# Expert stage of a fused model: float64 conversion on VectorE and ScalarE alone, its stores on SP's queue, row copies on ScalarE, another order of products and another branch form

## The chip, the cores and the metric

The kernel runs on one core of a Trainium2 chip. The metric is the device time of one execution in microseconds; less is better. Engines are named as in the profile: PE multiplies matrices, ACT is ScalarE, DVE is VectorE, POOL is GpSimd, and SP issues most DMAs. ACTq and SPq are the DMA queues that ACT and SP issue on, in the order of their own instructions.

## The reference

Three blocks follow each other: an attention with decay, a mixture of experts in which every token takes 2 of 8, and a gated product with large weights. `moe2_w_a` and its two companions arrive as float64.

```python
x = attention(q, k, v)                      # 1536 tokens, 512 wide
for e in range(8):                          # top 2 of 8 experts for each token
    mask = top2[:, k] == e
    out[mask] += top2_w[mask, k, None] * (np.maximum(x[mask] @ w1[e], 0.0) @ w2[e])   # 512 -> 1024 -> 512
a = x @ w_a                                 # 512 -> 1536, weights float64
b = x @ w_b
return (a * b @ w_out).astype(np.float32)
```

## The kernel before, in words

The attention and the choice of experts take the first 100 us or so. The expert stage, which the change is about, runs until about 450 us, and the gated product takes the rest.

**Products.** Every float32 factor is split into a high and a low part, and a product is three matmuls (`three`, lines 714 to 716): high by high, high by low, low by high. Weights are split as they come: `W.piece` (lines 81 and 82) copies half a unit to the high part on ACT (`whi`), subtracts on DVE (`wlo`), and then has SP load the next raw half. Two raw halves are in memory at a time.

**Experts.** The tokens of an expert are gathered into `xg`, transposed (`xprep`) and split (`xh`, `xl`). For each of 8 slices `f` of the hidden layer, `up` makes 12 matmuls into a PSUM tile `pu`, of which there are two; ACT writes the high part of the relu (`hh` or `hz`, line 747), DVE the low part (line 750). `down` multiplies that slice by the second weights and adds into four PSUM tiles `py0` to `py3`, which exist once. A list `behind` keeps `down` two slices behind `up`. So the last `down` of expert e-1 stands in slice 1 of expert e. Directly behind it `yevac` copies the four `py` tiles to `yt`: two on ACT (line 789), two on DVE (line 787). The next product is `up` of slice 2; the `down` after it writes `py0` again.  In slices 3 to 6 `ytrans` transposes `yt` and POOL scatters the rows to `ytab` in memory. In slice 6 POOL gathers the tokens of the expert after the next.

**Conversion.** Beside this the float64 weights are turned into float32, 36 chunks of 128 x 512: in slices 0, 1, 3, 5 and 7 of an expert, and in more slices of the first two. `wide_load` has SP fetch the words (`wr`). `wide_first` converts the low word on ACT (`wl`, line 592), and on DVE it works out the float32 word from the high one in six operations (lines 593 to 598). One slice later `wide_second` multiplies and adds the low part on POOL (lines 608 and 609), and one slice after that `wide_store` writes the chunk to `wtab` on ACT's queue (line 616). In expert 3, slice 1, SP also sends a list to memory and reads it back in another layout (`last_index`, lines 669 and 672); the second DMA waits for the first.

**Branch.** In expert 0, half of the tokens are worked ahead of a branch: `tc.If(rounds > 0)` (line 971) covers the case that an expert has more tokens than its tiles hold. With these data it isn't entered. All engines read `rounds` and branch.

The program's order is fixed by the code: each engine works its own list in order.

Of the kernel before, what the change touches and what calls it, by code (L numbers as in the profile page):

```python
# [8 lines left out]
F32 = mybir.dt.float32  # L9
# [3 lines left out]
U32 = mybir.dt.uint32  # L13
AF = mybir.ActivationFunctionType
OP = mybir.AluOpType
# [74 lines left out]
def tile_model(ctx: ExitStack, tc: tile.TileContext, q, k, v, w_gate, w_noise, noise, w1, w2,  # L90
               w_a, w_b, w_out, cst, tok, out):
    nc = tc.nc
# [12 lines left out]
    units, wide = [], []  # L105
# [457 lines left out]
    psu = mctx.enter_context(tc.tile_pool(name="psu", bufs=2, space=PSUM, reuse_waits="tile"))  # L563


    LO = float(np.uint32(896 << 20).view(np.float32))
    HI = float(np.uint32(1151 << 20).view(np.float32))
    wide_raw, wide_mid = {}, {}
    wide_n = [0, 0, 0, 0]

# [9 lines left out]
            return zp.tile([128, 512], U32, tag="zl", name="wa")  # L580
        return m2.tile([128, 512], U32, tag="wa", name="wa", bufs=3)

    def wide_first():

        n = wide_n[1]
        if n >= len(wide):
            return
        wr = wide_raw.pop(n)
        hw, lw = wr[:, :, 1], wr[:, :, 0]
        a = wide_word(n)  # L590
        q_, lf = (m2.tile([128, 512], U32, tag=x, name=x, bufs=2) for x in ("wq", "wl"))
        nc.scalar.activation(lf.bitcast(F32), lw, AF.Copy, scale=2.0 ** -52)
        nc.vector.tensor_scalar(a, hw, 0x7FFFFFFF, None, OP.bitwise_and)
        nc.vector.tensor_scalar(q_, hw, 0x7FFFFFFF, 0x3FFFFFFF, OP.bitwise_or, OP.bitwise_xor)
        nc.vector.tensor_scalar(a.bitcast(F32), a.bitcast(F32), LO, HI, OP.max, OP.min)
        nc.vector.tensor_scalar(a, a, 3, 0x7FFFFFFF, OP.logical_shift_left, OP.bitwise_and)
        nc.vector.tensor_tensor(a, a, q_, OP.bitwise_xor)
        nc.vector.tensor_scalar(q_, a, 0xFF800000, None, OP.bitwise_and)  # L598
        wide_mid[n] = (a, q_, lf)
        wide_n[1] += 1  # L600
        wide_load()

    def wide_second():
        n = wide_n[2]
        if n >= wide_n[1]:
            return
        a, q_, lf = wide_mid.pop(n)
        nc.gpsimd.tensor_tensor(lf.bitcast(F32), lf.bitcast(F32), q_.bitcast(F32), OP.mult)  # L608
        nc.gpsimd.tensor_tensor(a.bitcast(F32), a.bitcast(F32), lf.bitcast(F32), OP.add)  # L609
        wide_mid[n] = a  # L610
        wide_n[2] += 1

    def wide_store():
        n = wide_n[3]
        if n < wide_n[2]:
            nc.scalar.dma_start(wide[n][1], wide_mid.pop(n).bitcast(F32))
            wide_n[3] += 1


# [54 lines left out]
    XG, XH, XL, HH, HL, PY, YT, YS = {}, {}, {}, {}, {}, {}, {}, {}  # L674
# [54 lines left out]
    def up(e, f, w=None, keep=False, c=None, wait=False):  # L729
        if not w:  # L730
            v = slice(f % 4 * 128, f % 4 * 128 + 128)
            w = [[x[:, d, v] for d in range(4)] for x in W.tiles[("w1", e, f // 4)]]
        wh, wl = w
        a, b = c or (0, cap(e))
        n = b - a
        pu = psu.tile([128, 512], F32, tag="pu", name="pu")[:, 0:n]
        for d in range(4):
            three(pu, wh[d], wl[d], XH[e][:, d, a:b], XL[e][:, d, a:b], d == 0, d == 3)
        if keep:
            if f % 4 == 0:  # L740
                last[f // 4] = last_half(f // 4)
            HH[e, f], HL[e, f] = last[f // 4][0][f % 4], last[f // 4][1][f % 4]
        elif e == "r":
            HH[e, f], HL[e, f] = (m2.tile([128, 512], U32, tag="wl", name="wl").bitcast(F32R)[:, 0:n] for _ in range(2))
        else:
            HH[e, f], HL[e, f] = hidden(n)
        nc.scalar.activation(HH[e, f], pu, AF.Relu)  # L747

        def low():
            nc.vector.scalar_tensor_tensor(HL[e, f], pu, 0.0, HH[e, f].bitcast(F32), OP.max, OP.subtract)  # L750

        if wait:
            return low
        low()
# [27 lines left out]
    def yevac(e):  # L782
        YT[e] = m1.tile([128, 4, CP], F32, tag="yt", name="yt")
        n = cap(e)
        for m in range(4):
            if m % 2:
                nc.vector.tensor_copy(YT[e][:, m, 0:n], PY[e][m][:, 0:n])
            else:
                nc.scalar.copy(YT[e][:, m, 0:n], PY[e][m][:, 0:n])  # L789

    def scatter(ix, src):
        nc.gpsimd.indirect_dma_start(out=ytab, out_offset=bass.IndirectOffsetOnAxis(ap=ix, axis=0),
# [47 lines left out]
    def count_rounds():  # L840


        cnt = ranks["cnt"]
        nc.vector.tensor_tensor(rr[:, 0:E], cnt, caps, OP.is_gt)
        nc.vector.tensor_tensor(early[:, 1:E], early[:, 1:E], ranks["sel"][0:1, E - 2], OP.mult)
        nc.vector.tensor_reduce(rr[:, 8:9], rr[:, 0:E], AX.X, OP.max)
        nc.vector.tensor_reduce(early[:, 0:1], early[:, 1:E], AX.X, OP.add)
        nc.vector.tensor_reduce(rr[:, 9:10], cnt, AX.X, OP.max)
        nc.vector.scalar_tensor_tensor(rr[0:1, 8:9], few, PA - OFF, rr[0:1, 8:9], OP.is_lt, OP.max)
        nc.vector.scalar_tensor_tensor(rr[0:1, 8:9], early[:, 0:1], 128.0 - OFF, rr[0:1, 8:9], OP.is_gt, OP.max)  # L850
        for i in range(NR):
            nc.vector.tensor_scalar(rr[0:1, i:i + 1], rr[0:1, 9:10], i * CP - OFF, rr[0:1, 8:9], OP.is_gt, OP.mult)
        with nc.allow_low_precision(reason="whole numbers up to 4"):
            nc.vector.tensor_reduce(ri32, rr[0:1, 0:NR], AX.X, OP.add)
# [108 lines left out]
    up(0, 0, c=gb)  # L963
    nc.vector.memset(pofs, -float(CP))
    count_rounds()
    up(0, 1, c=gb)
    down(0, 0, c=gb)
    up(0, 2, c=gb)
    down(0, 1, c=gb)
    rounds = load_rounds()  # L970
    with tc.If(rounds > 0, preferred_fallthrough_block=False):
        more_rounds(rounds)
    xtiles("r")
    W.piece()
# [10 lines left out]

    for e in range(E):
        for f in range(0 if e else 3, NF):
            wide_store()
            wide_second()
            if e == E - 1:  # L990
                up(e, f, keep=True)
            else:
                up(e, f)
                behind.append((e, f))
            if e and 3 <= f < 7:
                ytrans(e - 1, f - 3)
            if behind and (len(behind) > 2 or e == E - 1):
                next_down()
            if e + 1 < E and 0 <= f - 2 - (e == 0) < 4:
                xprep(e + 1, f - 2 - (e == 0))  # L1000
            if e + 2 < E and f == 6:
                gather(e + 2)
            if e == E - 1 and f > 1:
                tile_mm(e, 0, f - 2)
            if e == 2 and f == 1:
                gate()
            if e == 3 and f == 1:
                last_index()
            if e + 1 < E:
                if e or f > 1:  # L1010
                    W.piece()
                if f in (0, 1, 3, 5, 7) or e < 2 and f == 4 or e == 0 and f == 6:
                    wide_first()
            elif f < 6:
                W.piece()
    G0 = [sum(GS[:i]) for i in range(len(GS))]
    YG, X2, ZH, ZL = {}, {}, {}, {}

# [188 lines left out]
```

## Time and profile before

| | |
|---|---|
| median of 3 runs | 790.31 us (787.67 to 790.79) |
| profiled execution | 789.01 us, of which its span is 787.2 us |
| granted TensorE clock, mean | 0.97 |

The span goes from the first to the last instruction; 1.8 us lie around it. The profile gives for each engine its busy time, in windows the clock that TensorE was granted (1.00 is 2.4 GHz, 0.50 is 1.2 GHz), and for each instruction how long its engine stood idle before it and which instruction released it. Line numbers are those of the kernel before.

### The profile page before, as it was taken

Reading aid. Unit: us, or ns where it says so; the run is one execution under the profiler, and the core shown is the slowest. Engines: PE = TensorE matmul, PEld = TensorE weight load, DVE = VectorE, ACT = ScalarE, POOL = GpSimd, SP = SyncE. Lnnn points to the kernel's source line nnn. Section 1 sums busy time; section 2 is a strip of 40 time slices with the busy share of each in tenths; the row PEclk is TensorE's granted clock in tenths of the full one; section 3 lists DMA queues with packets and bytes.
Section 4 is the critical chain, followed back from the end, with each engine's and each line's share of the span. In section 5 each row is a group of like instructions: output and inputs, shape, how many; then the busy total and the mean of one; then the engine's idle time right before and its main releaser. Section 6 shows DMA issues by size and latency. Waiting matters only on the chain. (4 is left out here: it accounts for less than half of the span.)

```text
span 787.2 us, 12000 instructions
## 1 busy us (share of the span) xinstructions
PE 735.6 (93%) x4657; PEld 683.8 (87%) x4657; DVE 433.6 (55%) x800; ACT 281.7 (36%) x524; POOL 215.1 (27%) x164
## 2 busy tenths in 40 slices
PE   8989898979899898979899979999999999999997
PEld 5878787869799887979889859999999999999997
DVE  4587565989778679787887534632222332222211
ACT  3674723335443343535344534421112122111211
POOL 4331131655746446474654210000000000000000
PEclk9999998989999899999999988999999999999999
DMA  9894244776857568576765654602001202000100
GB/s 219 224 263 117 56 143 142 234 214 221 247 200 232 165 216 253 201 235 219 235 211 164 180 188 155 188 1 81 0 1 41 81 1 81 1 1 1 41 1 27
DMA packets 85997, 107.85 MB, mean 137 GB/s; under 512 B 34521, under 2 KB 48089, under 8 KB 85934
## 3 DMA queue, kind: packets, MB, share of 16 engines
q1 hardware_dynamic: 69054, 81.45, 34.5%
q0 software_dynamic: 6272, 13.32, 5.9%
q10 hardware_dynamic: 10608, 12.25, 4.5%
q8 instruction: 38, 0.62, 0.3%
q14 instruction: 25, 0.20, 0.1%
HBM read 84.60 MB, written 22.38 MB: 136 GB/s over the span
## 5 line engine op out<-in xcount | busy, mean ns | idle before, releaser
L714 PE MATMUL ab<-zh,whi 128*128 128x256 f32 (+1 forms) x480 | 146.7, 306 | 0.0
L716 PE MATMUL ab<-zh,wlo 128*128 128x256 f32 (+1 forms) x480 | 146.6, 305 | 0.0
L715 PE MATMUL ab<-zl,whi 128*128 128x256 f32 (+1 forms) x480 | 146.5, 305 | 0.0
L82 DVE TENSOR_TENSOR wlo<-raw,whi 128x1024 fp32r<-128x1024 f32 x82 | 120.1, 1466 | 37.8 <-ACT whi L81 34.3
L1104 DVE TENSOR_TENSOR gf<-ab,bs 128x256 f32<-128x256 f32 (+1 forms) x60 | 28.6, 477 | 179.5 <-PE ab L716 179.4
L714 PE MATMUL pu<-xh,whi 128*128 128x432 f32 (+9 forms) x268 | 96.1, 358 | 7.4 <-issue 3.8
L714 PEld LDWEIGHTS ab<-zh,whi 128*128 128x128 f32 x480 | 92.0, 192 | 2.6
L715 PEld LDWEIGHTS ab<-zl,whi 128*128 128x128 f32 x480 | 91.9, 192 | 2.4
L81 ACT CAST whi<-raw 128x1024 fp32r<-128x1024 f32 x82 | 86.3, 1053 | 18.3 <-DMA raw<-wtab 9.9
L715 PE MATMUL pu<-xl,whi 128*128 128x432 f32 (+9 forms) x268 | 92.6, 346 | 0.0
L716 PE MATMUL pu<-xh,wlo 128*128 128x432 f32 (+9 forms) x268 | 92.4, 345 | 0.0
L716 PEld LDWEIGHTS ab<-zh,wlo 128*128 128x128 f32 x480 | 91.9, 191 | 0.0
L608 POOL TENSOR_TENSOR wl<-wl,wq 128x512 f32<-128x512 f32 x36 | 47.3, 1315 | 100.4 <-DVE wq L598 87.3
L609 POOL TENSOR_TENSOR wa<-wa,wl 128x512 f32<-128x512 f32 x36 | 72.8, 2023 | 2.8
L714 PE MATMUL py<-hh,whi 128*128 128x408 f32 (+8 forms) x160 | 59.3, 370 | 13.6 <-ACT yt L789 8.6
L1103 ACT COPY bs<-ab 128x256 f32<-128x256 f32 (+1 forms) x60 | 24.9, 415 | 122.2 <-PE ab L716 122.2
L1105 ACT CAST gh<-gf 128x256 fp32r<-128x256 f32 (+1 forms) x60 | 27.0, 449 | 107.6 <-DVE gf L1104 107.6
L714 PEld LDWEIGHTS pu<-xh,whi 128*128 128x128 f32 x268 | 52.0, 194 | 9.6 <-issue 4.0
L747 ACT ACTIVATE hh<-pu 128x408 fp32r<-128x408 f32 (+9 forms) x42 | 20.8, 496 | 105.3 <-POOL wa L609 40.6
L714 PE MATMUL po<-whi,gh 128*128 128x512 f32 x144 | 57.9, 402 | 0.0
L715 PE MATMUL py<-hl,whi 128*128 128x408 f32 (+8 forms) x160 | 56.8, 355 | 0.0
L715 PE MATMUL po<-wlo,gh 128*128 128x512 f32 x144 | 56.7, 394 | 0.0
(212 smaller groups left out, 1383.6 us busy)
## 6 DMA issues: line engine op xcount, KB each, us to landing
raw<-in_moe_w SPq DMA_DIRECT2D x64, 512.0 KB, 4.0
wtab<-wa ACTq DMA_DIRECT2D x36, 256.0 KB, 4.1
raw<-wtab SPq DMA_DIRECT2D x18, 512.0 KB, 4.2
wr<-in_moe_w_a SPq DMA_DIRECT2D x12, 512.0 KB, 5.3
wr<-in_moe_w_b SPq DMA_DIRECT2D x12, 512.0 KB, 5.1
wr<-in_moe_w_out SPq DMA_DIRECT2D x12, 512.0 KB, 6.5
yg<-ytab SPq DMA_DIRECT2D x24, 256.0 KB, 3.7
kr<-in_k SPq DMA_DIRECT2D x12, 256.0 KB, 5.1
```

Source lines behind the costliest of these rows:

```text
L81: nc.scalar.copy(hi[:, a:b], raw)
L82: nc.vector.tensor_tensor(lo[:, a:b], raw, hi[:, a:b].bitcast(F32), OP.subtract)
L608: nc.gpsimd.tensor_tensor(lf.bitcast(F32), lf.bitcast(F32), q_.bitcast(F32), OP.mult)
L609: nc.gpsimd.tensor_tensor(a.bitcast(F32), a.bitcast(F32), lf.bitcast(F32), OP.add)
L714: nc.tensor.matmul(ps, ah, bh, start=start, stop=False, skip_group_check=part)
L715: nc.tensor.matmul(ps, ah, bl, start=False, stop=False, skip_group_check=part)
L716: nc.tensor.matmul(ps, al, bh, start=False, stop=stop, skip_group_check=part)
L747: nc.scalar.activation(HH[e, f], pu, AF.Relu)
L1103: nc.scalar.copy(bs, ps["b"])
L1104: nc.vector.tensor_tensor(gf, ps["a"], bs, OP.mult)
L1105: nc.scalar.copy(GH[g, f][:, 0:n], gf)
```

## The change

- The conversion: ACT takes the absolute value of the high word as a float, scaled (`AF.Abs`, into `wa`), and converts the low word as before. DVE has six operations: sign, minimum, shift and or, mask, and the product and the sum that POOL made. POOL has none. All of it stands in one slice (`wide_convert`).
- The stores go to SP's queue, behind `W.piece` of the next slice, instead of ACT's queue at the start of a slice.
- `yevac` makes its four copies on ACT.
- Ahead of the branch the same five products stand as up 0, up 1, up 2, down 0, down 1; before it was up 0, up 1, down 0, up 2, down 1.
- The branch loses `preferred_fallthrough_block=False`.

```diff
-    LO = float(np.uint32(896 << 20).view(np.float32))
-    HI = float(np.uint32(1151 << 20).view(np.float32))
+    HI = float(np.uint32((254 << 20) + 0xFFFFF).view(np.float32))
...
-        nc.scalar.activation(lf.bitcast(F32), lw, AF.Copy, scale=2.0 ** -52)
-        nc.vector.tensor_scalar(a, hw, 0x7FFFFFFF, None, OP.bitwise_and)
-        nc.vector.tensor_scalar(q_, hw, 0x7FFFFFFF, 0x3FFFFFFF, OP.bitwise_or, OP.bitwise_xor)
-        nc.vector.tensor_scalar(a.bitcast(F32), a.bitcast(F32), LO, HI, OP.max, OP.min)
-        nc.vector.tensor_scalar(a, a, 3, 0x7FFFFFFF, OP.logical_shift_left, OP.bitwise_and)
-        nc.vector.tensor_tensor(a, a, q_, OP.bitwise_xor)
-        nc.vector.tensor_scalar(q_, a, 0xFF800000, None, OP.bitwise_and)
-        wide_mid[n] = (a, q_, lf)
+        nc.scalar.activation(a.bitcast(F32), hw.bitcast(F32), AF.Abs, scale=2.0 ** -112)
+        nc.scalar.activation(lf.bitcast(F32), lw, AF.Copy, scale=2.0 ** -52)
+        nc.vector.tensor_scalar(s, hw, 0x80000000, None, OP.bitwise_and)
+        nc.vector.tensor_scalar(a.bitcast(F32), a.bitcast(F32), HI, None, OP.min)
+        nc.vector.scalar_tensor_tensor(a, a, 3, s, OP.logical_shift_left, OP.bitwise_or)
+        nc.vector.tensor_scalar(s, a, 0xFF800000, None, OP.bitwise_and)
+        nc.vector.tensor_tensor(lf.bitcast(F32), lf.bitcast(F32), s.bitcast(F32), OP.mult)
+        nc.vector.tensor_tensor(a.bitcast(F32), a.bitcast(F32), lf.bitcast(F32), OP.add)
+        wide_mid[n] = a
...
-        nc.gpsimd.tensor_tensor(lf.bitcast(F32), lf.bitcast(F32), q_.bitcast(F32), OP.mult)
-        nc.gpsimd.tensor_tensor(a.bitcast(F32), a.bitcast(F32), lf.bitcast(F32), OP.add)
...
-            nc.scalar.dma_start(wide[n][1], wide_mid.pop(n).bitcast(F32))
+            nc.sync.dma_start(wide[n][1], wide_mid.pop(n).bitcast(F32))
...
-            if m % 2:
-                nc.vector.tensor_copy(YT[e][:, m, 0:n], PY[e][m][:, 0:n])
-            else:
-                nc.scalar.copy(YT[e][:, m, 0:n], PY[e][m][:, 0:n])
+            nc.scalar.copy(YT[e][:, m, 0:n], PY[e][m][:, 0:n])
...
     up(0, 1, c=gb)
+    up(0, 2, c=gb)
     down(0, 0, c=gb)
-    up(0, 2, c=gb)
     down(0, 1, c=gb)
     rounds = load_rounds()
-    with tc.If(rounds > 0, preferred_fallthrough_block=False):
+    with tc.If(rounds > 0):
...
         for f in range(0 if e else 3, NF):
-            wide_store()
-            wide_second()
...
                     W.piece()
+                wide_store()
                 if f in (0, 1, 3, 5, 7) or e < 2 and f == 4 or e == 0 and f == 6:
-                    wide_first()
+                    wide_convert()
             elif f < 6:
                 W.piece()
+                wide_store()
```

The first place is ACT's list in slices 0 and 1 of expert 3, where the products of expert 2 (416 columns) are copied. In brackets stand the engines and DMA lanes that a row waits for. Before:

```order
L81 CAST whi<-raw 128x1024 [waits DMAHW0_49]
L592 ACTIVATE wl<-wr 128x512 [waits DMAHW6_49]
L616 DMA wtab<-wa 128x512 [waits DMAHW3_49,Pool_49]
L747 ACTIVATE hh<-pu 128x408 [waits DVE_49,PE_49]
L789 COPY yt<-py 128x416 [waits PE_49] x2
L81 CAST whi<-raw 128x1024 [waits DMAHW1_49]
L592 ACTIVATE wl<-wr 128x512 [waits DMAHW2_49]
```

And with the change:

```order
L81 CAST whi<-raw 128x1024 [waits DMAHW7_49]
L592 ACTIVATE wa<-wr 128x512 [waits DMAHW6_49,DMAHW0_49]
L593 ACTIVATE wl<-wr 128x512 [waits DVE_49]
L738 ACTIVATE hh<-pu 128x408 [waits DVE_49,PE_49]
L777 COPY yt<-py 128x416 [waits PE_49] x4
L81 CAST whi<-raw 128x1024 [waits DMAHW1_49]
L592 ACTIVATE wa<-wr 128x512 [waits DMAHW4_49,DMAHW2_49]
L593 ACTIVATE wl<-wr 128x512 [waits DVE_49]
```

The store, which waited for POOL, is gone from between the conversion and the relu `hh`; the absolute value (`wa<-wr`) has come in ahead of the low word's conversion; and four copies stand where two stood.

The second place is SP's list in slice 1 of expert 3, with the load of raw weights, the load of a float64 chunk and the list that goes to memory. Before:

```order
L111 ISA x2
L63 ISA
L63 DMA raw<-in_moe_w 128x2x512 [waits DMAHW0_49,DVE_49]
L575 DMA wr<-in_moe_w_b 128x1024 [waits DMAHW6_49,DVE_49,Activation_49]
L669 DMA lst<-idy 108x4x1
L672 DMA idl<-lst 128x1 [waits DMAHW6_49]
```

And with the change:

```order
L111 ISA x2
L63 ISA
L63 DMA raw<-in_moe_w 128x2x512 [waits DMAHW7_49,DVE_49]
L607 DMA wtab<-wa 128x512 [waits DMAHW4_49]
L574 DMA wr<-in_moe_w_b 128x1024 [waits DMAHW6_49,DVE_49,Activation_49]
L660 DMA lst<-idy 108x4x1
L663 DMA idl<-lst 128x1 [waits DMAHW6_49]
```

The store of the chunk before stands directly behind the load of raw weights, whose wait for DVE is a later one than its own, and ahead of the next chunk's load.

The third place is the end of PE's list ahead of the branch: the last matmuls of down 1, the read of `rounds`, and the branch. Before:

```order
L715 MATMUL py<-hl,whi 128x212
L716 MATMUL py<-hh,wlo 128x212
L857 TENSOR_LOAD ri_1236 [waits DVE_49]
L971 COMPARE_AND_BRANCH
L971 UNCONDITIONAL_BRANCH [waits PE_49]
L892 COMPARE_AND_BRANCH
```

And with the change:

```order
L706 MATMUL py<-hl,whi 128x212
L707 MATMUL py<-hh,wlo 128x212
L845 TENSOR_LOAD ri_1236 [waits DVE_49]
L960 COMPARE_AND_BRANCH
L880 COMPARE_AND_BRANCH
```

The jump that waited for PE's own matmuls (`UNCONDITIONAL_BRANCH [waits PE_49]`) is gone; the comparison itself now jumps over the block. L892 before and L880 now are the first rows of the block that isn't entered.

## Rows read from the trace of the kernel before

**Rows 1.** The page's part 1: busy time of each engine over the span

```profile
PE 735.6 (93%) x4657; PEld 683.8 (87%) x4657; DVE 433.6 (55%) x800; ACT 281.7 (36%) x524; POOL 215.1 (27%) x164
```

**Rows 2.** Windows: busy us by engine, granted clock, DMA share, GB/s

```profile
240.00:250.00 10.00, 10.00 (x56) 9.96 (x54) 7.35 (x12) 4.58 (x7) 8.20 (x7) 1.00 0.75 250
250.00:260.00 10.00, 6.69 (x33) 5.98 (x32) 9.86 (x14) 2.82 (x5) 6.77 (x6) 0.92 0.99 287
```

**Rows 3.** Waits of PE, 126 to 450 us: total, times, longest

```profile
PE py L714 <- ACT yt L789: 14.6, 7, 3.1
PE py L714 <- DVE yt L787: 6.8, 6, 1.4
PE pu L714 <- DVE hz L750: 2.5, 1, 2.5
...
PE pu L714 <- DVE hl L750: 1.1, 1, 1.1
```

**Rows 4.** Timeline of PE: start, duration, operation, idle before it

```profile
252.62 0.35 PE L714 MATMUL pu<-xh,whi 128*128 128x408 f32 x1
...
254.66 0.35 PE L716 MATMUL pu<-xh,wlo 128*128 128x408 f32 x1
256.91 0.46 PE L714 MATMUL py<-hh,whi 128*128 128x408 f32 x1 [1.91 <-ACT yt L789]
...
259.14 0.71 PE L714 MATMUL py<-hh,whi 128*128 128x408 f32 x1 [1.40 <-DVE yt L787]
```

**Rows 5.** Timeline of ACT (ACTq: its queue), 248 to 257 us

```profile
248.72 0.67 ACT L592 ACTIVATE wl<-wr 128x512 f32<-128x512 uint32 x1
255.53 0.33 ACTq L616 DMA_DIRECT2D wtab<-wa  x1
...
256.36 0.91 ACT L789 COPY yt<-py 128x416 f32<-128x416 f32 x2
```

**Rows 6.** Timeline of POOL, 253 to 256 us

```profile
253.34 2.15 POOL L609 TENSOR_TENSOR wa<-wa,wl 128x512 f32<-128x512 f32 x1
```

**Rows 7.** Groups by line, DVE, 126 to 450 us: busy us, mean ns

```profile
L82 DVE TENSOR_TENSOR wlo<-raw,whi 128x1024 fp32r<-128x1024 f32 x59 | 90.3, 1530 | 17.5 <-ACT whi L81 17.5
L593 DVE TENSOR_SCALAR wa<-wr 128x512 uint32<-128x512 uint32 x36 | 29.2, 810 | 0.0
L597 DVE TENSOR_TENSOR wa<-wa,wq 128x512 uint32<-128x512 uint32 x36 | 25.0, 696 | 1.2
```

**Rows 8.** Line L593 alone: duration in ns, minimum/median/maximum

```profile
L593 DVE TENSOR_SCALAR wa<-wr x36: 411/421/1515, 130.8 to 427.6; 128x512 uint32<-128x512 uint32 x36
```

**Rows 9.** Groups by line and form, DVE, 474 to 787 us

```profile
L82 DVE TENSOR_TENSOR wlo<-raw,whi 128x1024 fp32r<-128x1024 f32 x11 | 13.5, 1223 | 5.4 <-ACT whi L81 5.4
...
L1027 DVE SCALAR_TENSOR_TENSOR yg<-yg,wts 128x512 f32<-128x512 f32 x10 | 7.5, 752 | 0.4
```

**Rows 10.** Groups by line, ACT, 126 to 450 us

```profile
L81 ACT CAST whi<-raw 128x1024 fp32r<-128x1024 f32 x59 | 62.3, 1056 | 9.8 <-DMA raw<-in_moe_w 5.1 <-DMA raw<-wtab 4.7
L592 ACT ACTIVATE wl<-wr 128x512 f32<-128x512 uint32 x36 | 24.6, 683 | 0.0
```

**Rows 11.** Windows of the six half-clock stretches at expert turns, their sum

```profile
sum 26.70, PE 23.80 PEld 22.30 DVE 26.13 ACT 9.05 POOL 18.29; mean PE 3.97 PEld 3.72 DVE 4.35 ACT 1.51 POOL 3.05
```

**Rows 12.** Timeline of PE at the branch, 118 to 123 us

```profile
118.48 0.27 PE L716 MATMUL py<-hh,wlo 128*128 128x212 f32 x1
122.58 0.72 PE L714 MATMUL pu<-xh,whi 128*128 128x428 f32 x1 [3.83 <-issue]
```

**Rows 13.** Line L971, the branch: ns, minimum/median/maximum, PE's sequencer

```profile
L971 PEldq COMPARE_BRANCH  x2: 95/1840/3584, 117.2 to 118.9; - x2
```

**Rows 14.** Window of the half-clock stretch behind the branch

```profile
121.90:128.70 6.80, 6.12 (x19) 5.65 (x20) 1.69 (x3) 1.11 (x3) 0.00 (x0) 0.50 0.53 189
```

**Rows 15.** Waits of SP's queue, 126 to 450 us

```profile
SPq L672 <- DMA lst<-idy: 10.7, 1, 10.7
```

**Rows 16.** Line L575, the loads of float64 chunks: time to landing

```profile
DMA to landing us min/median/max: 4.1/5.8/10.2
```

More of the change, by code (lines that the diff above doesn't have):

```diff
@@ L581, in wide_word, with wide_convert @@
         return m2.tile([128, 512], U32, tag="wa", name="wa", bufs=3)
-    def wide_first():
+    def wide_convert():
         n = wide_n[1]
@@ L590, in wide_first @@
         a = wide_word(n)
-        q_, lf = (m2.tile([128, 512], U32, tag=x, name=x, bufs=2) for x in ("wq", "wl"))
+        s, lf = (m2.tile([128, 512], U32, tag=x, name=x, bufs=2) for x in ("wq", "wl"))
+        nc.scalar.activation(a.bitcast(F32), hw.bitcast(F32), AF.Abs, scale=2.0 ** -112)
         nc.scalar.activation(lf.bitcast(F32), lw, AF.Copy, scale=2.0 ** -52)
-        nc.vector.tensor_scalar(a, hw, 0x7FFFFFFF, None, OP.bitwise_and)
-        nc.vector.tensor_scalar(q_, hw, 0x7FFFFFFF, 0x3FFFFFFF, OP.bitwise_or, OP.bitwise_xor)
-        nc.vector.tensor_scalar(a.bitcast(F32), a.bitcast(F32), LO, HI, OP.max, OP.min)
-        nc.vector.tensor_scalar(a, a, 3, 0x7FFFFFFF, OP.logical_shift_left, OP.bitwise_and)
-        nc.vector.tensor_tensor(a, a, q_, OP.bitwise_xor)
-        nc.vector.tensor_scalar(q_, a, 0xFF800000, None, OP.bitwise_and)
-        wide_mid[n] = (a, q_, lf)
+        nc.vector.tensor_scalar(s, hw, 0x80000000, None, OP.bitwise_and)
[5 more added lines that the diff above has]
+        wide_mid[n] = a
         wide_n[1] += 1
         wide_load()
[L603 to L607, printed above, removed]
-        nc.gpsimd.tensor_tensor(lf.bitcast(F32), lf.bitcast(F32), q_.bitcast(F32), OP.mult)
-        nc.gpsimd.tensor_tensor(a.bitcast(F32), a.bitcast(F32), lf.bitcast(F32), OP.add)
-        wide_mid[n] = a
-        wide_n[2] += 1
     def wide_store():
         n = wide_n[3]
-        if n < wide_n[2]:
-            nc.scalar.dma_start(wide[n][1], wide_mid.pop(n).bitcast(F32))
+        if n < wide_n[1]:
+            nc.sync.dma_start(wide[n][1], wide_mid.pop(n).bitcast(F32))
             wide_n[3] += 1
```

## The prediction, as made before the run

> **What bounds the kernel now.** I read the page's busy times first: PE is busy 93% of the span, no other engine over 55% [rows 1]. So time can be won only where PE stands still or runs at half clock. The windows show where. In 240 to 250 us PE is busy throughout; in 250 to 260, where expert 3 takes over from expert 2, it is busy 6.69 of 10 us, with DVE at 9.86 and the DMA engines at 0.99 [rows 2]. Next I asked for PE's waits over the whole expert stage: 14.6 us for `yt` on ACT in 7 waits, 6.8 us for `yt` on DVE in 6, and 2.5 and 1.1 us for a low part (`hz`, `hl`) on DVE [rows 3]. So the turn from one expert to the next is the main loss, 21.4 us, and the early conversions, 3.6 us, the second.
>
> The timelines of one turn tell why. PE ends the `up` of slice 2 at 254.7 + 0.35, and the first matmul of the next `down` comes at 256.91, after 1.91 us of waiting for ACT; the second `py` tile costs another 1.40 us, for DVE, at 259.14 [rows 4]. ACT ended a conversion at 248.72 + 0.67 = 249.39 and did nothing until its store was issued at 255.53; relu and `yt` copies stood behind it [rows 5]. The store waited for POOL's sum, which ran from 253.34 to 255.49 [rows 6]. So ACT, needed by PE, stood 6.1 us behind POOL.
>
> DVE is held up by POOL as well. The split `wlo` takes 1530 ns on average here [rows 7] but 1223 ns in the last stage, where POOL has almost nothing to do [rows 9]; L593 averages 810 ns [rows 7] with a median of 421 and a maximum of 1515 [rows 8]. These two lines alone hold 59 x 0.307 + 36 x 0.389 = 32 us of excess.
>
> **The change, part by part.** The sum is made against the profiled execution, 789.0 us, 1.3 us under the median of 790.3; that difference is within the spread of the runs.
>
> *POOL's two operations and ACT's store go.* ACT's block at each turn falls away, and with it the wait for the first copy. Two copies on ACT take 0.91 us [rows 5], so 0.46 each, and PE needs three matmuls, 0.56 us, for each `py` tile (12 matmuls from 252.62 to 254.85 are 2.2 us [rows 4]), so one engine's copies keep ahead of PE; besides, PE has the `up` of slice 2 to do while they run, 2.2 us. The second wait, for DVE, goes because DVE makes no copy. Gain: 14.6 + 6.8 = 21.4 us.
>
> *The clock.* After the branch and after six turns TensorE is granted 0.50 of its clock. The windows of the six turns add up to 23.80 us of PE work at 0.50 [rows 11], which at full clock takes half: 11.9 us. Each of these stretches comes right after a turn's idle time. If it goes, they go. Gain: 11.9, the lower bound being 0 if as much idle time appears elsewhere.
>
> *DVE's new load.* Per chunk, sign, minimum and mask are taken at L593's 0.42, product and sum at L597's 0.70 (two inputs in memory, 512 columns), and the shift with or, which the trace does not show, lies between that 0.70 and the 0.75 of L1027, an operation of the same class [rows 7 to 9]. I take 0.75: 3.41 us. The old six, undisturbed, are five of 0.42 and one of 0.70, 2.80. So +0.6 x 36 = 22 us, against 32 us of excess that goes with POOL and some 6 us for 14 copies. DVE is relieved on balance, but unevenly: a slice with a conversion costs it 1.22 + 3.41 + at most 0.70 for `hl` = 5.3 us, against 4.4 us on PE (two products of 2.2). Slices 7, 0 and 1 convert in a row: 2.7 us of backlog. In the first two experts it is seven in a row, four of them with `xl` (at most 6.0 us against 5.1 with transposes and 428 columns) and three without (5.3 against 4.7): at most 5.4 us. PE feels a backlog only when `pu` runs out, which is after three products, 6.6 us. So the early waits go too, narrowly. Gain: 3.6; between 0 and 3.6.
>
> *ACT's new load.* 36 absolute values, for which the conversion of the low word stands (0.683 [rows 10]; both read a strided 128 x 512), and 14 copies, 25 + 6 = 31 us, less 36 issues of stores of 0.33 us. The fullest slice holds 4.8 us of work: the split 1.06 [rows 10], two conversions 1.37, a relu, taken like a copy, 0.5, and four copies 1.8. That is 0.4 over PE's 4.4, once per expert, and covered by the same three products; if that cover went, it would cost 0.7 us at each conversion.
>
> *The stores on SP.* They stand behind the raw load, whose wait on DVE is the later one, so they add no wait, only 0.33 us of issue each. But a turn's 20 us move 250 and 287 GB/s [rows 2], and 287 at a share of 0.99 is what the DMA engines give. Taking 4.8 us (turn and clock) out of that stretch asks for 5.4 MB in 15.2 us, 353 GB/s. Raw halves and chunks are fetched two slices ahead, so the surplus can spread over neighbouring slices, not vanish. I charge 3 us in all (0 to 13).
> SP also waits 10.7 us once, in expert 3, for the list that it reads back [rows 15], and the stores now queue with the loads behind it. PE, no longer delayed just before, runs into the late weights: 2 us (0 to 5).
>
> The Trainium skill, page DMA: Bandwidth & Descriptors, section Issuing engines are not separate DMA queues, says that the issuing engine makes no difference to the transfer and that only its issue time is saved. By that rule moving the stores is worth 12 us of ACT's issue time, none of it on the path, so 0; by the rows, what is saved is the wait in front of the issue, which no transfer contains.
>
> *Branch and order.* PE's last matmul ahead of the branch ends at 118.75, the next starts at 122.58 after 3.83 us of "issue" [rows 12]. Of the two comparisons on PE's sequencer the first takes 95 ns at 117.2, while matmuls still run; the second, the jump that had waited for them, takes 3584 ns at 118.9 [rows 13]. With the change the first one is the jump. If it lasts as long, PE goes on at 117.2 + 3.6 = 120.8: 1.8 us earlier, which I round to 1.7. Bounds: 0, if the jump starts no earlier, and 2.7, if the new order lets PE's sequencer run further ahead. The half clock behind it [rows 14] I leave, since 2 us of idle time remain.
>
> The Trainium skill, page Runtime: NRT & Kernel Launch, section Instruction fetch mechanics, holds that a taken jump out of the fetched window waits for a fetch. By that rule the jump costs as much as before, and only its earlier start counts, the same 1.7.
>
> Sum: 21.4 + 11.9 + 3.6 + 1.7 - 3 - 2 = 33.6, so 755.4 us, and I predict 755.
>
> **The rivals.**
>
> *DMA or DVE sets the pace at the turns* (0.23). The stretch of 5.4 MB can't go under 18.7 us at 287 GB/s, which leaves 1.3 of the 4.8 us per turn; with the same backlog DVE, at its upper prices, passes the 6.6 us. For it: DMA share 0.99 and DVE 9.86 in that window. Against: buffers two slices ahead, and DVE's share there holds POOL's excess. Half of turns and clock stay away: 755 + 16 = 771, or, mildly, 763 to 771.
>
> *All of it, and more* (0.13). The two debits don't come, and the half clock behind the branch goes as well, 6.12 / 2 = 3.1 [rows 14]: 755.4 - 5 - 3.1 = 747. For it: the single waits of 2.5 us elsewhere in the stage.
>
> *Copies come, the clock doesn't return, or the gains cancel* (0.04): within 0.5% of now, about 789. It needs new idle time of 34 us; nothing shows that much.
>
> *Slower: the absolute value blocks ACT* (0.04). It stands ahead of relu on ACT and waits for a chunk's load, which is issued when the conversion two chunks before has read its buffer, some 9 us earlier in a run of converting slices. Landing takes 5.8 us at the median and 10.2 at most [rows 16]. The low word's conversion had the same wait, so it is no new one; but with stores on the same queue loads may come later. It decides from about 9 + 6.6 = 15 us of landing: beyond that each microsecond holds PE at up to 36 conversions. At 17 us, 72 us would be lost against 34 won: about 827; at 16, 791.
>
> **How the numbers follow.** The forecast's own case (748 to 762) has 0.56. The range that leaves no more than 2 in 10 out reaches from the upper rival's 746 to the DMA rival's 771. About 0.5% (4 us) is what a measurement of this kernel can tell from no change: faster 0.92, same 0.04, slower 0.04.
>
> **What would show it.** Right: no store on ACT's queue; ACT's `yt` copies right behind the relu of slice 1; PE's waits for `yt` under 3 us in total; the granted clock at 1.00 from the first turn to 450 us; the mean of `wlo` in the stage near 1.23 us; PE idle for about 2 us at the branch. Wrong: PE waiting for `hl` or for `xl` in the first two experts (DVE's price too low), ACT's `whi` or `wa` waiting for DMA for more than some 15 us (DMA sets the pace), or PE idle around expert 3, slices 3 to 5, for more than 5 us.

## The result, and the profile after

The changed kernel takes 754.9 us (median of 4 runs, 750.53 to 755.97); beside it on the same chip the kernel before took 789.96 us. The ratio is 0.955, with a 95% interval of 0.951 to 0.959: faster. The prediction was 755.0. Line numbers below are those of the changed kernel, if not said otherwise; its profiled execution took 755.97 us, its span 754.2 us.

The page's part 1 after the change:

```profile
PE 721.5 (96%) x4657; PEld 675.2 (90%) x4657; DVE 404.8 (54%) x786; ACT 311.6 (41%) x574; POOL 105.6 (14%) x92
```

Against [rows 1], POOL's work is halved, ACT has 30 us more, DVE 29 us less, and PE's share of the span rises to 96%. PE's busy time falls by 14 us for the same matmuls, mostly because fewer of them run at half clock.

The waits of PE from 122 to 420 us (total, times, longest), which answer to [rows 3]:

```profile
PE ptr L687 <- DMA xg<-xtab,idx: 8.7, 3, 6.8
PE pu L705 <- DVE hl L741: 0.6, 1, 0.6
```

No wait for `yt` is left. The timeline of ACT at the turn from expert 2 to 3 shows why (compare [rows 5]):

```profile
232.40 0.51 ACT L738 ACTIVATE hh<-pu 128x408 fp32r<-128x408 f32 x1 [1.91 <-PE pu L707]
232.96 2.21 ACT L777 COPY yt<-py 128x416 f32<-128x416 f32 x4
```

The relu waits for PE, no longer for a store, and the four copies stand right behind it. The windows (busy us of PE, PEld, DVE, ACT, POOL, then granted clock, DMA share, GB/s) show the clock:

```profile
121.00:124.50 3.50, 3.50 (x13) 3.16 (x12) 0.00 (x0) 0.28 (x1) 2.78 (x3) 0.51 0.68 204
200.00:240.00 40.00, 39.34 (x224) 38.51 (x222) 33.56 (x54) 23.06 (x38) 11.26 (x8) 1.00 0.79 246
244.00:251.00 7.00, 4.86 (x18) 4.62 (x18) 1.80 (x2) 1.70 (x3) 0.00 (x0) 0.52 0.15 26
251.00:420.00 169.00, 167.05 (x968) 162.49 (x966) 125.36 (x195) 96.19 (x159) 38.63 (x31) 1.00 0.73 235
```

The six half-clock stretches of [rows 11] are gone; one is left behind the branch, and a new one at 244 us follows PE's longest new wait. The groups by line from 122 to 420 us, first of DVE, then of ACT (busy us, mean ns), answer to [rows 7] and [rows 10]:

```profile
L82 DVE TENSOR_TENSOR wlo<-raw,whi 128x1024 fp32r<-128x1024 f32 x59 | 72.1, 1222 | 21.5 <-ACT whi L81 21.1 <-issue 0.3
L598 DVE TENSOR_TENSOR wl<-wl,wq 128x512 f32<-128x512 f32 x36 | 25.0, 695 | 3.7
...
L596 DVE SCALAR_TENSOR_TENSOR wa<-wa,wq 128x512 uint32<-128x512 uint32 x36 | 24.9, 692 | 1.2
```

```profile
L592 ACT ACTIVATE wa<-wr 128x512 f32<-128x512 f32 x36 | 24.3, 675 | 5.7 <-DMA wr<-in_moe_w_b 2.9 <-DMA wr<-in_moe_w_a 2.5 <-DMA wr<-in_moe_w_out 0.2
...
L777 ACT COPY yt<-py 128x428 f32<-128x428 f32 (+6 forms) x28 | 13.5, 509 | 1.1
```

At the branch (compare [rows 12]) PE stands idle for 2.61 us instead of 3.83:

```profile
117.38 0.27 PE L707 MATMUL py<-hh,wlo 128*128 128x212 f32 x1
120.26 0.43 PE L705 MATMUL pu<-xh,whi 128*128 128x428 f32 x1 [2.61 <-PEq L960]
```

The new wait stands in expert 3, behind the list of [rows 15]. The timelines of POOL, SP and PE:

```profile
232.34 1.23 POOL L679 DMA_INDIRECT xg<-xtab,idx  x1 [0.30 <-issue]
```

```profile
232.62 0.52 SPq L660 DMA_DIRECT2D lst<-idy  x1
246.29 1.20 SPq L663 DMA_DIRECT2D idl<-lst  x3
```

```profile
246.14 0.39 PE L687 MATMUL ptr<-cs,xg 76*128 76x76 f32 x1 [6.80 <-DMA xg<-xtab,idx]
```

POOL issues the last tile of a gather at 232.34, SP the list 0.28 us later, and both land at about 246 us, so PE waits 6.80 us for that tile. The other 1.9 us of the 8.7 for gathers are two waits at 326 and 328 us, far from the list.

**Ledger of the two profiled executions**, 789.01 - 755.97 = 33.0 us. Turns 21.4 [rows 3]; early waits for DVE 3.6 - 0.6 = 3.0; branch 3.83 - 2.61 = 1.2; half clock 11.9 at the turns [rows 11], (6.12 - 3.50) / 2 = 1.3 behind the branch [rows 14], less 4.86 / 2 = 2.4 for the new stretch; two smaller waits of before, for `ys` and `xl`, 1.9; less 8.7 for gathers. That is 29.6. PE's idle time fell by (787.2 - 735.6) - (754.2 - 721.5) = 18.9 us, and the waits above make 18.8 of it, so the other 3.4 us lie in PE's busy time. A part belongs to the waits themselves: ahead of a wait the last matmul runs out alone, 0.35 us, where matmuls that follow each other start 0.19 us apart [rows 4]. For 13 waits fewer that is an estimate of 13 x 0.16 = 2.1 us; the rest stays open.

### The profile page after: what moved, and what is told of

Same layout as the page of the kernel before. It is cut to its first block, busy times and chain, and to the rows that moved or that the text cites. A ratio compares the mean times of both kernels' runs of the same rounds, so it can differ in the third digit from the quotient of the medians.

```text
span 754.2 us, 11955 instructions
## 1 busy us (share of the span) xinstructions
PE 721.5 (96%) x4657; PEld 675.2 (90%) x4657; DVE 404.8 (54%) x786; ACT 311.6 (41%) x574; POOL 105.6 (14%) x92
## 5 line engine op out<-in xcount | busy, mean ns | idle before, releaser
L82 DVE TENSOR_TENSOR wlo<-raw,whi 128x1024 fp32r<-128x1024 f32 x82 | 101.2, 1235 | 42.7 <-ACT whi L81 38.4
L1092 ACT COPY bs<-ab 128x256 f32<-128x256 f32 (+1 forms) x60 | 24.9, 416 | 122.0 <-PE ab L707 122.0
L780 POOL DMA_INDIRECT ytab<-ys,idy x28 | 33.7, 1202 | 231.1 <-ACT ys L789 161.1
L707 PE MATMUL po<-whi,gl 128*128 128x512 f32 x144 | 56.5, 393 | 0.0
L705 PE MATMUL py<-hh,whi 128*128 128x408 f32 (+8 forms) x160 | 55.9, 349 | 0.0
L706 PE MATMUL py<-hl,whi 128*128 128x408 f32 (+8 forms) x160 | 54.5, 341 | 0.0
L707 PE MATMUL py<-hh,wlo 128*128 128x408 f32 (+8 forms) x160 | 54.5, 341 | 0.0
```

Source lines behind the costliest of these rows:

```text
L82: nc.vector.tensor_tensor(lo[:, a:b], raw, hi[:, a:b].bitcast(F32), OP.subtract)
L705: nc.tensor.matmul(ps, ah, bh, start=start, stop=False, skip_group_check=part)
L706: nc.tensor.matmul(ps, ah, bl, start=False, stop=False, skip_group_check=part)
L707: nc.tensor.matmul(ps, al, bh, start=False, stop=stop, skip_group_check=part)
L1092: nc.scalar.copy(bs, ps["b"])
```

## The experiments

The theory: the turns cost what they did because a store on ACT's queue waited for POOL's sum, and because two of the four copies stood behind a DVE that POOL slowed; removing both gives the turns and their clock back. The rivals: one of these alone is enough, the DVE excess that goes with POOL is worth nothing to PE, and the branch is worth nothing that can be measured. Runs of one of these kernels scatter over 3 to 8 us, so waits are read from the profiles and totals only compared where intervals part; a time inside or outside an expected range by a few us says little.

**e1_copies_only.** The kernel before, with the copies of the change.

```diff
-            if m % 2:
-                nc.vector.tensor_copy(YT[e][:, m, 0:n], PY[e][m][:, 0:n])
-            else:
-                nc.scalar.copy(YT[e][:, m, 0:n], PY[e][m][:, 0:n])
+            nc.scalar.copy(YT[e][:, m, 0:n], PY[e][m][:, 0:n])
```

> The kernel before with one edit: all four copies of yevac on ACT. First theory (the turn is lost because ACT stands behind its store, which waits for POOL): the wait for DVE's copy, 6.8 us, goes, but the wait for ACT's first copy, 14.6 us in 7 waits, stays, and so does most of the half clock behind the turns; 778 to 785 us. Rival (sharing the copies with a late DVE is the cause): the waits at the turn go together with the half clock, 33 us; 757 to 765 us.

Measured: 788.07 us, ratio 0.9998 (0.9971 to 1.0026). PE's waits, 115 to 430 us:

```profile
PE py L714 <- ACT yt L786: 15.3, 6, 3.3
PE ptr L796 <- ACT ys L798: 6.4, 7, 1.8
```

The 6.8 us for DVE are gone, and 6.4 us for `ys` on ACT (1.3 before) and 3.3 us for `xl` (0.6 before) have come in their place. The first theory has the waits right, but not its 778 to 785 us. While ACT is stuck behind the store, moving the copies to it is worth nothing.

**e2_stores_only.** The kernel before, with the stores on SP's queue.

```diff
-            nc.scalar.dma_start(wide[n][1], wide_mid.pop(n).bitcast(F32))
+            nc.sync.dma_start(wide[n][1], wide_mid.pop(n).bitcast(F32))
```

> The kernel before with one edit: the stores of converted chunks are issued on SP's queue at the same place of the program; POOL still makes product and sum, DVE still makes two of four copies. First theory (ACT's block behind POOL causes the first wait): PE's wait for ACT's copy falls from 14.6 to under 4 us, the wait for DVE's copy stays near 6.8 us or grows, half of the clock loss returns, and SP's raw loads now stand behind POOL, which may cost a few us: 765 to 775 us. Rival (POOL's hold on DVE is the cause, not the store's queue): DVE is as late as before and the wait for ACT's copy turns into one for DVE or for weights; 783 to 792 us.

Measured: 773.29 us, ratio 0.980 (0.976 to 0.983). PE's waits:

```profile
PE py L714 <- DVE yt L787: 5.4, 3, 3.1
PE ptr L696 <- DMA xg<-xtab,idx: 5.4, 6, 1.4
...
PE pu L714 <- DVE hz L750: 3.0, 2, 2.5
PE pu L714 <- DVE hl L750: 2.4, 2, 1.5
```

All 14.6 us for ACT are gone with one line of code, as the first theory has it, and the time is in its range. But the gain, 15 us beside the 788.51 us of the kernel before on the same chip, is less than half of the change's 35: DVE's waits stay, and gathers begin to be late.

**e14_copies_and_stores.** The kernel before, with both edits above.

> The kernel before with two parts of the change: all four row copies on ScalarE, and the stores on SP's queue; the conversion keeps its product and sum on GpSimd, and the branch is as before. Theory (the rival that held where product and sum went back to GpSimd): once no store stands ahead of ScalarE's copies and no slowed VectorE operation ahead of the others, the turns' waits are gone; with the old branch and the early waits that remain, the time is 758 to 764 us. Rival: VectorE's longer conversion still matters through waits for the hidden tiles' low parts; then TensorE waits for VectorE by 4 us or more between 150 and 420 us, and the time is 765 to 772 us.

Measured: 772.88 us, ratio 0.981 (0.977 to 0.985): no better than the stores alone. PE's waits:

```profile
PE ptr L696 <- DMA xg<-xtab,idx: 12.7, 10, 2.3
...
PE pu L714 <- DVE hz L750: 3.0, 2, 2.5
PE pu L714 <- DVE hl L750: 2.7, 3, 1.5
```

The theory's 758 to 764 falls. PE waits for DVE by more than the rival's 4 us (7.1 between 150 and 420 us, for `hz`, `hl` and `xl`), with the time 0.9 us above its range; but the largest wait, for gathers, the rival didn't name. The `yt` waits are gone, and late gathers take their place. POOL issues them behind its own product and sum, where it waits for DVE's `wq` (line 598 of before). POOL's wait, its issue of the last tile of one gather, and PE's first matmul on that expert's tokens:

```profile
POOL wl L608 <- DVE wq L598: 72.7, 23, 18.3
205.44 0.96 POOL L688 DMA_INDIRECT xg<-xtab,idx  x1 [0.30 <-issue]
209.51 0.26 PE L696 MATMUL ptr<-cs,xg 108*128 108x108 f32 x1
```

Before, POOL waited longer still, 87.3 us, but the two times were 206.08 and 217.63: with the turns' waits gone PE comes 8 us sooner, and POOL hardly does. That POOL's wait for DVE makes the gather late is read from these rows; no run tried it by itself.

**e8_pool_math.** The changed kernel, with product and sum back on POOL.

```diff
-        nc.vector.tensor_tensor(lf.bitcast(F32), lf.bitcast(F32), s.bitcast(F32), OP.mult)
-        nc.vector.tensor_tensor(a.bitcast(F32), a.bitcast(F32), lf.bitcast(F32), OP.add)
+        nc.gpsimd.tensor_tensor(lf.bitcast(F32), lf.bitcast(F32), s.bitcast(F32), OP.mult)
+        nc.gpsimd.tensor_tensor(a.bitcast(F32), a.bitcast(F32), lf.bitcast(F32), OP.add)
```

> The changed kernel with product and sum of the conversion on POOL instead of DVE; stores stay on SP's queue, where they now wait for POOL, and all copies on ACT. First theory (beside the block of ACT, POOL's hold on DVE costs time of its own): the mean of the split wlo goes back to about 1.5 us, PE waits for low parts and SP's loads come late behind POOL; 760 to 772 us. Rival (only the block of ACT counted; DVE's excess is off the path, and DVE has 1.4 us less per chunk to do): 751 to 757 us.

Measured: 756.44 us, ratio 0.958 (0.954 to 0.961). DVE's groups from 150 to 420 us:

```profile
L82 DVE TENSOR_TENSOR wlo<-raw,whi 128x1024 fp32r<-128x1024 f32 x55 | 86.4, 1571 | 39.2 <-ACT whi L81 39.0
L596 DVE SCALAR_TENSOR_TENSOR wa<-wa,wq 128x512 uint32<-128x512 uint32 x32 | 23.2, 724 | 1.1
```

POOL slows `wlo` again, to 1571 ns, and PE hardly notices. Its waits behind the branch, 115 to 430 us, are these and 0.6 us for `xl`:

```profile
PE ptr L787 <- ACT ys L789: 3.6, 1, 3.6
PE ptr L687 <- DMA xg<-xtab,idx: 2.1, 4, 1.0
```

The time is in the rival's range. So beside the other edits, taking the two operations off POOL was not needed: in this kernel the four operations left on DVE cost 2.30 us a chunk (0.658 + 0.488 + 0.724 + 0.432), slowed as they are, and in e14 the six cost 3.61. POOL waits 56.0 us for `wq` in place of 72.7, and the two times of e14's gather are 195.43 and 201.73.

Three edits part this kernel's 756 from e14's 773: the new form of the sign and the exponent, with its absolute value on ACT; the branch, which e3 can't tell from the scatter; and the store's place on SP's list, ahead of the next chunk's load instead of behind it. The last doesn't look like the cause, since ACT waits no longer for loads in e14 than here (19.0 us against 24.9, 115 to 430 us, ahead of `whi` and the conversions). That leaves the new form, by elimination: no run has it alone.

**e6_stores_act.** The changed kernel, with the stores back on ACT's queue (one line, e2's the other way round).

> The changed kernel with the stores on ACT's queue, at the place that they have in the change. They wait for DVE's sum of the slice before, no longer for POOL. First theory (the wait for POOL was the harm, not the queue): ACT stands a few tenths of a us per store and PE's three products cover it; 753 to 758 us. Rival (any store on ACT holds up relu and copies): PE waits 1 to 3 us at each of 7 turns for ACT and half clock returns; 765 to 780 us.

Measured: 750.12 us, ratio 0.952 (0.947 to 0.958), below both ranges, though its runs (749.6 to 757.89) span all of the changed kernel's; no wait for `yt`. A store on ACT's queue costs nothing that can be seen as soon as it waits for DVE's sum in place of POOL's, at the place that it has in the change. The Trainium skill, page DMA: Bandwidth & Descriptors, section Issuing engines are not separate DMA queues, holds that the issuing engine makes no difference but for its issue time. This run agrees with it (0.952 beside 0.955), and e2 shows what it doesn't speak of: the wait that stands in front of an issue.

**e5_copies_split.** The changed kernel, with two of the four copies back on DVE (e1's the other way round).

> The changed kernel with two of four yevac copies back on DVE. First theory (DVE is on time once POOL no longer holds it): PE waits for a DVE copy at most 1 us per turn, no half clock returns; 754 to 759 us. Rival (copies on ACT are what ends the second wait): 6.8 us of waiting and the half clock behind it return; 764 to 775 us.

Measured: 756.93 us, ratio 0.960 (0.955 to 0.964). One wait for `yt` on DVE of 2.35 us came back, at the turn at 163.57, and one of 0.30. The time is in the first theory's range, but 2.35 is more than the 1 us that it allows at a turn. With the shorter conversion DVE's copies are late by more than 0.3 us only at the first turn, around which chunks follow each other in every slice.

**e3_branch_as_before.** The changed kernel, with the old order and the old form of the branch.

```diff
     up(0, 1, c=gb)
-    up(0, 2, c=gb)
     down(0, 0, c=gb)
+    up(0, 2, c=gb)
     down(0, 1, c=gb)
     rounds = load_rounds()
-    with tc.If(rounds > 0):
+    with tc.If(rounds > 0, preferred_fallthrough_block=False):
```

> The changed kernel with the branch form and the order of the five products of before. First theory: PE's idle time at the branch goes back from 2.6 to 3.8 us and the half clock behind it from 3.4 to 6.8 us, which is 1.2 + 1.5 = 2.7 us; everything else stays: 757 to 759 us. Rival (the branch part is worth nothing beyond the noise, since later waits take up what it gives): 754 to 756 us.

Measured: 754.64 us, ratio 0.956 (0.953 to 0.960). The idle time at the branch is back (3.59 us), and so is the 6.8 us stretch of half clock: 1.0 us of idle time, and at most 1.7 of clock. The total doesn't show it; behind the list PE waited 3.6 us here, for `ys` on ACT, and 6.8 us in the profiled run of the change, for a gather. That agrees with the rival, but 2.7 us can't be told from the scatter.

**e11_loads_ahead.** The changed kernel, with the first two chunk loads ahead of the branch.

```diff
+    for _ in range(2):
+        wide_load()
     rounds = load_rounds()
...
-    for _ in range(2):
-        wide_load()
```

> The changed kernel with the first two loads of the expert stage's chunks issued just ahead of the branch, where the change leaves them just behind it. Theory: the time that the branch gives is taken back because the first chunk's load lands late and holds ScalarE's Abs, with the first relus behind it; then TensorE's early waits (0.6 us on VectorE in the changed kernel, 3.0 us where the list was set apart) go to nothing in this kernel, and the time is 1 to 3 us shorter, 752 to 754 us. Rival: the small waits behind the branch are those of the first hidden tiles and not of the load; then an early wait of 0.6 us stays and the time is 754 to 756 us.

Measured: 754.88 us, ratio 0.956 (0.952 to 0.959). The early wait for `hl` is gone, as the theory has it, but the branch takes it back, and the time is in the rival's range. The jump on PE's sequencer, first in the changed kernel, then in this one, each with the window ahead of PE's return:

```profile
L960 PEldq COMPARE_BRANCH  x1: 3792/3792/3792, 116.3 to 116.3; - x1
```

```profile
117.00:119.00 2.00, 0.65 (x6) 0.47 (x5) 0.00 (x0) 0.19 (x1) 0.00 (x0) 1.00 0.15 33
```

```profile
L962 PEldq COMPARE_BRANCH  x1: 6292/6292/6292, 115.5 to 115.5; - x1
```

```profile
117.00:119.00 2.00, 0.04 (x1) 0.00 (x0) 0.00 (x0) 0.00 (x0) 0.00 (x0) 1.00 1.07 273
```

With the DMA engines full (share 1.07) the jump lasts 6.29 us, with them nearly empty (0.15) 3.79. The trace has the packets of the instruction queues too; the one of 16 KB there began 1.0 us after the jump in the changed kernel and 3.6 us after it here, and PE went on 1.6 and 2.5 us after its end:

```
kernel      jump    16 KB packet     PE goes on
changed     116.3   117.28-118.70    120.26
e11         115.5   119.10-120.42    122.87
e13         118.2   121.82-123.02    125.13
```

The Trainium skill, page Runtime: NRT & Kernel Launch, section Instruction fetch mechanics, holds that a taken jump out of the fetched window waits until its target has been fetched by DMA. These rows agree, and add that the fetch comes later with data under way; that this jump left the fetched window is not seen directly.

**e4_list_later.** The changed kernel, with the list at expert 3, slice 4.

```diff
-            if e == 3 and f == 1:
+            if e == 3 and f == 4:
```

> The changed kernel with the list of expert 7 sent to memory and read back in slice 4 of expert 3 instead of slice 1. First theory (the last tile of expert 4's gather, issued 0.3 us before the list's write, is held back by that write, which shares the DMA engines): PE's wait of 6.8 us for the gathered rows goes, and the half clock behind it with 2.3 us, while SP still waits 10 to 13 us and delays weights by 0 to 4 us: 744 to 750 us. Rival (the gather is late by itself, because the DMA engines are full at the turn): PE waits 5 to 7 us for the same tile as before; 753 to 757 us.

Measured: 750.53 us, ratio 0.952 (0.949 to 0.956). The wait of 6.80 us is gone; one of 2.56 for a later gather, one of 2.17 for `hl` at the first chunk and some under 1 us have come. The first theory holds for this wait; the time is just above its range, and not clear of the changed kernel's.

**e9_list_apart.** The changed kernel, with the list written at expert 3, slice 4, and read back two experts later, so that SP doesn't wait for it.

```diff
+        return lst
+
+    def last_index_back(lst):
...
-            if e == 3 and f == 1:
-                last_index()
+            if e == 3 and f == 4:
+                lst = last_index()
+            if e == 5 and f == 4:
+                last_index_back(lst)
```

> The changed kernel with the list of expert 7 written in slice 4 of expert 3, where no gather is under way, and read back in slice 4 of expert 5, so that SP does not wait for it. First theory (the list's write held the gather, and SP's wait of 13 us delayed loads): the 6.8 us and 2.3 us of half clock go, and the waits for gathered rows of expert 5 seen with the list in slice 4 (2.6 and 0.8 us) go too, because POOL and SP are not behind; 743 to 748 us. Rival (SP's wait costs nothing): as with the list in slice 4, 749 to 752 us.

Measured: 754.95 us, ratio 0.955 (0.951 to 0.958). The theory that SP's wait is the cost falls, and the time is above the rival's range too. Windows behind the list's write, which was issued at 255.04, and two issues of SP in them:

```profile
260.00:265.00 5.00, 5.00 (x32) 4.89 (x31) 2.29 (x4) 2.99 (x5) 0.00 (x0) 1.00 0.32 20
265.00:270.00 5.00, 5.00 (x29) 5.00 (x28) 3.19 (x6) 0.58 (x1) 0.07 (x1) 1.00 0.83 108
270.00:275.00 5.00, 5.00 (x29) 4.99 (x28) 2.14 (x3) 2.96 (x4) 0.92 (x1) 1.00 0.92 308
```

```profile
259.50 0.41 SPq L63 DMA_DIRECT2D raw<-in_moe_w  x1
259.95 3.41 SPq L607 DMA_DIRECT2D wtab<-wa  x1
```

With a load and a store issued, the transfers stall all the same (20 GB/s) and catch up later; a gather was then 2.50 us late at 289 us. The run also shows a small case of my slower rival. The first chunk's load behind the branch was late, and ACT's absolute value with it:

```profile
134.24 0.67 ACT L592 ACTIVATE wa<-wr 128x512 f32<-128x512 f32 x1 [6.09 <-DMA wr<-in_moe_w_a]
```

The relu queued behind it, and PE waited 3.03 us for `hl`.

**e12_list_last.** The changed kernel, with the list at expert 7, slice 2.

```diff
-            if e == 3 and f == 1:
+            if e == 7 and f == 2:
```

> The changed kernel with the last expert's list written and read back at expert 7, slice 2, in place of expert 3, slice 1. Theory: the list's write of 432 four-byte elements holds whatever transfers are under way when it is issued, and costs only where a gather or a chunk is among them; at slice 2 of the last expert neither is, so TensorE's wait for a gathered tile (6.8 us) and the smaller ones behind it (1.9 us) go, with the 3.4 us of half clock behind them, and the time is 745 to 749 us. Rival: there the write holds up a transfer of the last stage (a weight piece or a row tile) or the scatter waits for the list; then TensorE waits 2 to 7 us after 420 us, and the time is 750 to 756 us.

Measured: 754.44 us, ratio 0.956 (0.952 to 0.959): the rival, though PE's waits come at 411 and 417 us and not after 420. The timelines of SP and PE:

```profile
398.70 0.47 SPq L660 DMA_DIRECT2D lst<-idy  x1
409.03 1.20 SPq L663 DMA_DIRECT2D idl<-lst  x3
410.33 8.58 SPq L63 DMA_DIRECT2D raw<-wtab  x4
```

```profile
411.21 0.44 PE L705 MATMUL pu<-xh,whi 128*128 128x380 f32 x1 [3.33 <-DVE wq L741]
```

The gather in expert 3 is late by 1.79 us even without the list. At its new place the list holds the weights of the last stage: a load issued at 398.30, 0.40 us ahead of it, reached ACT only at 408.39, where 4.2 us is the median of these loads in the kernel before.

**e13_ahead_last_act.** The edits of e6, e11 and e12 together.

> The changed kernel with three edits: the stores of converted chunks on ScalarE's queue as before the change, the first two chunk loads ahead of the branch, and the list at expert 7, slice 2. Theory: with the converted words made on VectorE alone a store on ScalarE's queue no longer stalls ScalarE for long, and SP is free to issue loads; the edits add, and the time is 743 to 748 us. Rival: the three remove waits that overlap, or the late list costs at the end; then the time is 749 to 754 us, what the stores on ScalarE's queue or the later list gave alone.

Measured: 754.69 us, ratio 0.956 (0.953 to 0.960): its rival's case, 0.7 us above the range. The jump lasts 6.19 us as in e11, and the late list costs 6.0 us in two waits. I found no version that is faster than the changed kernel by more than the scatter; e4 and e6 have the lowest medians, with intervals that overlap its own.

## Why the prediction was right, point by point

**Turns, 21.4, and their clock, 11.9: right in size and place.** No wait for `yt` is left, and the clock is 1.00 from the first turn to 420 us but for 244 to 251. My share of the reason is only half right. The store behind POOL's sum was the block on ACT, as e1, e2 and e6 show. But I had the rest come from the two copies and from the slowdown by POOL. e14 has the copies moved and gains nothing over e2; e8 has the slowdown and loses nothing that can be measured. What was needed besides the stores was, by elimination, a shorter run of DVE operations for each chunk, and moving the first of them to ACT gives that with POOL still at work.

**DVE's new load: price right, credit wrong.** The shift with or takes 692 ns, just under the 0.70 to 0.75 that I allowed, so a chunk costs 3 x 0.423 + 3 x 0.693 = 3.35 us instead of 3.41; `wlo` fell to 1222 ns, as said. I set 32 us of POOL's excess against 22 us of new work. Both are there in DVE's busy time, but e8 shows that the trade is worth some 1.5 us of the total (756.4 against 754.9), inside the scatter.

**ACT's new load: right.** The absolute value takes 675 ns (estimated by 683), a copy 509 (taken as 460), and ACT's busy time rises by 30 us for an estimate of 31.

**Early waits, 3.6: 3.0 came.** **Branch, 1.7: 1.2 came**, and 1.3 of the clock behind it, which I had left in. The jump itself got no shorter (3792 ns, 3584 before [rows 13]); it starts earlier. e3 shows that the total can't tell.

**DMA bursts, -3 (0 to 13): at most -2 came.** The two waits for gathers at 326 and 328 us, 1.9 us, follow a window with the DMA engines at 0.99:

```profile
320.00:325.00 5.00, 5.00 (x31) 4.96 (x29) 4.11 (x8) 3.65 (x7) 0.00 (x0) 1.00 0.99 272
```

But the last tile there landed 8.7 us after its issue (318.77 to 327.51), where 8.8 is the median of this run's gathers and 7.7 that of the kernel before; so by the medians the fuller engines added about 1 us, and the rest is that PE comes sooner. My 287 GB/s is no fixed ceiling either: e9 has 5 us of 308 GB/s at a share of 0.92. At the other turns the surplus spread over the neighbouring slices (39.34 of 40 us busy from 200 to 240, DMA at 0.79), and the rival that DMA or DVE sets the pace there is out.

**The list, -2: the step that failed in size.** It cost 6.8 us of waiting and 2.4 us of clock in the profiled run; e12 shows that some 1.8 us of the wait would be there without it (PE wants the tile 7.0 us after its issue in both). I looked for late weights behind SP's wait; what was late was a gather on POOL, whose last tile was issued 0.28 us ahead of the list. In e3, e5, e6 and e8, where 4.8 to 6.2 us lie between the two, no gather around the list is later than 1 us, and PE waits 2.5 to 3.7 us for `ys` instead. So the size hangs on where the list falls. With this wait one of my signs of being wrong came: PE idle around expert 3 for more than 5 us. Another came without harm: ACT waited 13.7 + 5.7 us for DMA ahead of `whi` and `wa`, and PE had no wait for weights.

That the total is right to 0.1 us is luck: the runs scatter over 5 us, and errors cancel, debits of 5 us that cost 11 (8.7 + 2.4) in the profiled run, against 1.3 + 1.9 + 3.4 us of gains that the sum didn't have. **The slower rival** (ACT's absolute value waits for a load) happens, at the first chunk: 1.62 us in the changed kernel, 6.09 in e9. In the stage it costs ACT 5.7 us in all and is far from its threshold.

What stays open: the new conversion alone, with the stores and copies of before, was not run, nor e14 with the store at its new place, and neither was e14 with its gathers issued ahead of POOL's product and sum.

## What to carry to other kernels

A wait in front of an issue blocks all that is queued behind it on that engine: look at what a store or a gather waits for before asking what it moves, and on which engine. When one wait at a point is removed, the next one there (a copy, a gather, a low part) often takes most of the gain, so price an edit by what is late next, and try parts together as well as alone: here the stores alone gave 15 of 35 us, the copies nothing alone or on top, and the other 20 came only with the new conversion beside them. A total that fits says little about the terms when they are as large as the errors that cancel.

## What the runs showed of the hardware

A list of 432 elements of 4 bytes stalls other transfers. In the changed kernel its last packet ends at 240.77, yet it and the tile of the gather issued just ahead of it are complete only at about 246 us, 13.8 us after the tile's issue; in e12, with the list elsewhere, the same tile took 8.8. From 240 to 245 us the DMA engines are all but idle while PE stands still:

```profile
240.00:245.00 5.00, 0.00 (x0) 0.00 (x0) 1.22 (x3) 0.00 (x0) 0.00 (x0) 0.90 0.02 4
```

This row alone is no proof, since SP waits for the list and issues nothing from 233 to 246 us; in e9 SP doesn't wait, and the transfers that it issued stall too. In the kernels that read the list back at once, 10.1 to 14.0 us passed between the issue of the list and that of its reading; what happens between the last packet and that point no run shows. The other surprise is the jump on PE, which lasts 3.31 to 3.79 us in the twelve kernels with no load issued just ahead of it, and 6.19 and 6.29 in the two with two loads of 512 KB there.
